# A six-layer cross network on one core: five named buffers, output in halves, first weights ahead of stores, and VectorE's sums interleaved

## The chip, the cores and the metric

One Trainium2 chip, one core. The metric is the device time of the program in microseconds, lower is better. The kernel before took 2305.39 us (median of three runs, 2305.22 to 2308.65).

## The reference, cut to what matters

```python
# x0: 16384 x 1024, ws: 6 x 1024 x 1024, bs: 6 x 1024, all bf16
x = x0
for l in range(6):
    proj = jnp.einsum('bd,de->be', x, ws[l]) + bs[l]
    x = x0 * proj + x
return x
```

Each row of x goes through the six layers by itself, so rows can be taken in any grouping; within a group the layers follow one another.

## The kernel before, in words

**Tiles.** The state is kept transposed in SBUF, features on partitions. A *pair* is 1024 rows, as two blocks n = 0, 1 of 512 rows, and the 1024 features are two halves of 512 (index `dh` of the input, `eh` of the output). A pair's x0 is a tile `x0T` (128 x 2 x 8 x 512), its running state a tile `xst` of the same size (2 MB each). There are 16 pairs.

**The product.** For one pair and one layer, the 2 x 2 blocks of rows and features are multiplied in Strassen's and Winograd's way: seven half-size products in place of eight. They are numbered 1 to 7, and so are their weight tiles (512 KB each): 1, 2 and 4 are blocks of the layer's matrix as it is, 5, 6, 3 and 7 are sums and differences of blocks. On the other side stand differences of state blocks: `T13` (one instruction that makes T[5] and T[7]), `T2` = T[6], `T4` = T[4]. From round 1 on, products 2 and 4 are split once more in the same way (`inner`, with the transformed weights 8 and 9, and with `ti2` and `ti4` on the side of the state).

**Loops.** Rounds s = 0 to 7 take two pairs each, sides A and B. Within a round, layers l = 0 to 5, and within a layer a *step* for A, then a step for B. PE's order in a step of rounds 1 to 7 is: product 1 (16 matmuls of 512 columns; after the first four the few matmuls that the previous step left over, `defer`), the inner products of 2 mixed in, product 5, product 3, product 6 with the inner products of 4, product 7. A step of round 0 has no inner products.

**VectorE.** It makes T13, T2, T4, ti2 and ti4, the sums of products that are C1 (output half 0) and C2 (output half 1), and then multiplies by x0 (`MULT`) and adds the old state (`ADD`) into `xst`. The sums for output half 1 of a step come in the next step, in `trail`: they are the *trail* of pair Y while PE works on pair X. Before, the sums of output half 0 are ended within the step itself (`fin`, called at the step's end for n = 1). ScalarE only empties PSUM.

**Weights.** In round 0, raw blocks come from HBM (`load_raw`), VectorE makes the combinations (`combo`, lines 117 to 130), and each is also stored to a buffer `Lc` in HBM. Later rounds load all nine tiles of a layer, in the order 1, 2, 8, 5, 3, 6, 4, 9, 7, from the input (1, 2, 4) or from Lc. They lie in a ring of 11 tiles, `wring`. The steps of side B ask for the loads (`weights`, which calls `prefetch_upto`, lines 92 to 97): when B uses the weight at place i, the one at place i + 10 is issued, and it waits until PE has ended with the tile that it replaces. Steps of side A issue none.

**The queue.** But for four weight loads at the start, which ScalarE issues, all DMAs are issued by SP, in one order: weights, x0 of new pairs (`load_x0`, a transposing DMA, line 198), and output. At the end of a pair `store_out` (line 248) transposes the 2 MB of state by one DMA back into the pair's own `x0T` tile (line 250), and then two DMAs of 1 MB write it to HBM in pieces of 256 bytes (line 254). `pin` keeps an instruction in the order in which the code gives it; what isn't pinned (before: weight loads, x0 loads, output and the stores to Lc) is placed by the scheduler. x0 tiles come from a pool of three, `xst` tiles from a pool of two. x0 of a new A pair is asked for at layer 2 of the round before, that of a new B pair in the step of A at layer 0 of its own round.

**The end.** The last pair isn't stored by DMA transposes: PE transposes its tiles, ScalarE and VectorE empty PSUM, and eight DMAs of 256 KB leave (`rows_out`, line 523).

Of the kernel before, what the change touches and what calls it, by code (L numbers as in the profile page):

```python
# [8 lines left out]
ADD = mybir.AluOpType.add  # L9
# [8 lines left out]
def kernel(  # L18
# [14 lines left out]
    NB = 512  # L33
# [28 lines left out]
    x0t_pool, xst_pool = pool("x0t", 3), pool("xst", 2)  # L62
# [4 lines left out]
    def wtile():  # L67
        return wring.tile([P, KH, H], BF16, name="wp")

# [20 lines left out]
    state = {"next": 0, "last_dma": None}  # L90

    def prefetch_upto(n):
        while state["next"] < min(n, len(keys)):
            k = keys[state["next"]]
            W[k] = wtile()
            state["last_dma"] = nc.sync.dma_start(W[k][:], raw_src(k[1], k[2]) if k[2] in RAW else lc(k[1], k[2]))
            state["next"] += 1

    def nosync(ins, before, reason):
        tc.add_manual_dep(ins.ins, before.ins.name,  # L100
                          mybir.DependencyInfo(mybir.DependencyClass.NoSync, mybir.DependencyReason.DATA),
                          reason=reason)

    raw12 = {}

    def load_raw(l, eng, pids):
        for pid in pids:
            if pid == 12:
                t = raw12[l] = ei_pool.tile([P, KH, H], BF16, name="ea")
            else:  # L110
                t = W[0, l, pid] = wtile()
            pin(eng.dma_start(t[:], raw_src(l, pid)))

    def combo(l, pid):
        if pid <= 7:
            a, op, b = {5: (lambda: raw12[l], ADD, lambda: W[0, l, 4]), 6: (lambda: W[0, l, 5], SUB, lambda: W[0, l, 1]),
                        3: (lambda: W[0, l, 2], SUB, lambda: W[0, l, 6]), 7: (lambda: W[0, l, 1], SUB, lambda: raw12[l])}[pid]
            t = ei_pool.tile([P, KH, H], BF16, name=("eb", "e4")[l % 2]) if pid == 5 else wtile()
            vtt(t[:], a()[:], b()[:], op)
            W[0, l, pid] = t  # L120
# [9 lines left out]
        nc.sync.dma_start(lc(l, pid), t[:])  # L130
# [4 lines left out]
    def inner_t(src, name):  # L135
        ti = ti_pool.tile([P, 4, 2, NQ], BF16, name=name)
        b = sub4(src)
        vtt(ti[:, 0], b[0, 1], b[0, 0], SUB)
        vtt(ti[:, 2], b[1, 1], b[0, 1], SUB)
        vtt(ti[:, 1], b[1, 1], ti[:, 0], SUB)  # L140
        vtt(ti[:, 3], b[1, 0], ti[:, 1], SUB)
        return ti
# [42 lines left out]
    x0T_A = x0t_pool.tile([P, 2, KD, NB], BF16, name="x0T")  # L185
    x0T_B = x0t_pool.tile([P, 2, KD, NB], BF16, name="x0T")
    xrows = [evt(), evt()] + [t_pool.tile([P, KH, NB], BF16, name=i) for i in ("T2", "T4")]
    for q in range(4):
        n, h = q // 2, q % 2
        pin(nc.sync.dma_start(xrows[q][:], x0[n * NB:(n + 1) * NB, h * H:(h + 1) * H].rearrange("(r p) d -> p r d", p=P)))  # L190
        if q == 0:
            pin(nc.sync.dma_start(b_rows[:], bs.rearrange("l (m p) -> (l m) p", p=P)))
    load_raw(0, nc.scalar, (1, 2, 12, 4))

    def load_x0(pr, x0T):
        for n in range(2):
            r0 = pr * PR + n * NB
            ti_ = nc.sync.dma_start_transpose(out=x0T[:, n], in_=x0[r0:r0 + NB, :])  # L198
            if state["last_dma"] is not None:
                nosync(ti_, state["last_dma"], "behind the weight loads already issued")  # L200

    load_x0(1, x0T_B)
    warm_in = const.tile([P, 1], BF16, name="warm_in")
# [25 lines left out]
    def trail(Y, prompt):  # L229

        if Y is None:
            return []
        C2 = Y.C2
        x0T, dst, src = Y.x0T, Y.xst, Y.src_in
        eh1 = lambda t: t[:, :, KH:KD, :]
        out = [lambda: vtt(C2[:, 1], Y.U3s[:], Y.P5s[:], ADD)]
        if Y.E4 is not None:
            def s4():
                e = Y.E4
                for i in range(2):  # L240
                    vtt(e[:, 2 * i:2 * i + 2, NQ:NB], e[:, 2 * i:2 * i + 2, (1 - i) * NQ:(2 - i) * NQ], Y.e5[:], ADD)
            out.append(s4)
            out.append(lambda: vtt(C2[:, 0], C2[:, 0], Y.E4[:], ADD))
        out.append(lambda: vtt(C2[:], C2[:], eh1(x0T), MULT))
        out.append(lambda: vtt(eh1(dst), C2[:], eh1(src), ADD))
        return out

    def store_out(Y):
        xo = Y.x0T[:].rearrange("p n k (j r) -> p (n k j) r", r=P)
        nc.sync.dma_start_transpose(out=xo, in_=Y.xst[:].rearrange("r n k b -> r (n k b)"))  # L250
        with nc.allow_non_contiguous_dma(reason="256B runs"):
            for n in range(2):
                r0 = Y.pr * PR + n * NB
                nc.sync.dma_start(out[r0:r0 + NB, :].rearrange("(j p) (k r) -> p k j r", p=P, r=P),  # L254
                                  Y.x0T[:, n].rearrange("p k (j r) -> p k j r", r=P))

    for s in range(NPAIR // 2):
        for l in range(L):
            for side in ("A", "B"):
# [6 lines left out]
                if l == 0:  # L266
                    X.xst = xst_pool.tile([P, 2, KD, NB], BF16, name="xst")
                if side == "A" and l == 0 and s > 0:
                    t = x0t_pool.tile([P, 2, KD, NB], BF16, name="x0T")
                    load_x0(X.pr + 1, t)  # L270
                    new["B"] = Pair(X.pr + 1, t)
                if side == "A" and l == 2 and s + 1 < NPAIR // 2:
                    t = x0t_pool.tile([P, 2, KD, NB], BF16, name="x0T")
                    load_x0(X.pr + 2, t)
                    new["A"] = Pair(X.pr + 2, t)

# [27 lines left out]
                half = lambda pt: (lambda m: pt[:, m * NQ:(m + 1) * NQ])  # L304
# [10 lines left out]
                todo = trail(Y, False)  # L315
# [10 lines left out]
                prompt = Y is not None and Y.l == L - 1  # L326
                own = []
                if not first:
                    own = [X.T2, X.T4]
                    if in4:  # L330
                        own.append(lambda: setattr(X, "ti4", inner_t(X.T[4], "ti4")))
                seq = todo + own if prompt else [f for pair in zip(todo + [None] * 9, own + [None] * 9) for f in pair if f is not None]
                for f in seq:
                    f()
                if prompt:
                    store_out(Y)
                if in2:
# [11 lines left out]
                    inner(half(q1), wr[0, 0], b[0, 0], True)  # L349
                    evi(ea[0, 0], q1)  # L350
                    inner(half(q5), wi[:, 0], ti[:, 0], True)
# [3 lines left out]
                    inner(half(q2), wr[1, 0], b[1, 0], True)  # L355
# [4 lines left out]
                    inner(half(q1), wi[:, 1], ti[:, 1], False)  # L360
                    evi(ea[0, 1], q1)
                    inner(half(q5), wi[:, 2], b[1, 1], False)
# [3 lines left out]
                    inner(half(q1), wi[:, 3], ti[:, 2], False)  # L366
                    evi(ea[1, 1], q1)
                    mm(5, w5, pX, 2, True)
                    inner(half(q1), wr[1, 1], ti[:, 3], False)
                    evi(ea[1, 0], q1)  # L370
                    ev(P5s, pX, 1)
                    ev(P5s, pX, 2)
                    w3 = weights(3)
# [11 lines left out]
                else:  # L385
# [24 lines left out]
                    for m in range(KH):  # L410
                        mm(5, w5, pX, m, True)
                        ev(P5s, pX, m)
                    w3 = weights(3)
# [17 lines left out]
                if need2 and not late:  # L431
                    N.ti2 = inner_t(N.rhs(2), "ti2")
                x0T, dst, src = X.x0T, X.xst, X.src

                def fin(Cb, eh, n):
                    xs = slice(eh * KH, (eh + 1) * KH)
                    vtt(Cb[:, n], Cb[:, n], x0T[:, n, xs, :], MULT)
                    return lambda: vtt(dst[:, n, xs, :], Cb[:, n], src[:, n, xs, :], ADD)

                fin(C1, 0, 0)()  # L440
                if s == 0:
                    if side == "A":
                        if l + 1 < L:
                            load_raw(l + 1, nc.sync, (12, 4, 1, 2))
# [10 lines left out]
                X.E4 = X.defer = None  # L455
                C2 = cb_pool.tile([P, 2, KH, NB], BF16, name="cb")
                X.C2, X.U3s, X.P5s, X.l, X.src_in = C2, U3s, P5s, l, src
                if in4:
# [9 lines left out]
                    inner(half(z1), wr4[0, 0], b4[0, 0], True)  # L468
# [3 lines left out]
                    inner(half(z5), wj[:, 0], t4[:, 0], True)  # L472
# [3 lines left out]
                    inner(half(z1), wj[:, 1], t4[:, 1], False)  # L476
# [5 lines left out]
                    inner(half(z1), wj[:, 3], t4[:, 2], False)  # L482
# [32 lines left out]
                fin(C1, 0, 1)()  # L515
                if need2 and late:
                    N.ti2 = inner_t(N.rhs(2), "ti2")
                if last:
                    final_tail = (X, C1, C2, U3s, P5s, psA, psX)
# [3 lines left out]
    X, C1, C2, U3s, P5s, psA, psX = final_tail  # L523
    def rows_out(pts, srcs, start, yo, n, eh, eng):
        for j in range(KH):
# [6 lines left out]
            if j % 2 == 1:  # L532
                r0 = X.pr * PR + n * NB + (j - 1) * P
                nc.sync.dma_start(out[r0:r0 + 2 * P, eh * H:(eh + 1) * H].rearrange("(j p) d -> p j d", p=P), yo[:, j - 1:j + 1, :])

    of_x = lambda n, eh: (lambda m, j: X.xst[:, n, eh * KH + m, j * P:(j + 1) * P])
    for h in range(2):
        hs = slice(2 * h, 2 * h + 2)
        vtt(C2[:, 1, hs, :], U3s[:, hs, :], P5s[:, hs, :], ADD)
# [5 lines left out]
    rows_out([bank(psX) for _ in range(KH)], of_x(0, 0), True, evt(), 0, 0, (1, 1, 1, 1))  # L545
    pT = [bank(psA) for _ in range(KH)]
    rows_out([bank(psX) for _ in range(KH)], of_x(1, 0), True, evt(), 1, 0, (1, 1, 1, 1))
# [33 lines left out]
```

## Time and profile before

| what | value |
|---|---|
| median of three runs | 2305.39 us |
| the profiled execution | 2303.93 us, its span 2302.1 us, mean granted clock 0.997 |
| PE, VectorE (DVE), ScalarE (ACT) busy | 98%, 95%, 83% of the span |
| matmuls of product 1 to 7 (L295), of inner products (L301) | 7829 of 512 columns, 4676 of 256 columns recorded |
| evictions of PSUM by ACT, 128 x 512 | 694 ns with bias, about 590 ns without |
| VectorE sums, 128 x 2048 and 128 x 4096 | 1.22 us, 2.29 us |
| DMA on SP's queue | 326.16 MB, 50.4% of 16 engines' span |
| weight load from Lc, from the input: issue to landing, median | 4.0 us, 5.3 us |
| output, 1 MB: issue to landing, median | 9.6 us |
| transposing DMA: x0 (1 MB), state (2 MB): issue to landing, median | 7.9 us, 11.7 us |

How to read it: busy shares are means over the whole span. Lines such as L46 or L295 are lines of helpers through which all sums or all matmuls go, so a group is known by its tiles: `T<-xst` is a difference of state blocks, `cb` a sum (C1 or C2), `wp` a weight, `px` PSUM. "SPq" is SP's sequencer, which issues DMAs. Some matmul records are missing, and a matmul's row lasts longer (379 ns) than the distance to the next one's start (216 ns).

### The profile page before, as it was taken

Reading aid. Unit: us, or ns where it says so; the run is one execution under the profiler, and the core shown is the slowest. Engines: PE = TensorE matmul, PEld = TensorE weight load, DVE = VectorE, ACT = ScalarE, POOL = GpSimd, SP = SyncE. Lnnn points to the kernel's source line nnn. Section 1 sums busy time; section 2 is a strip of 40 time slices with the busy share of each in tenths; the row PEclk is TensorE's granted clock in tenths of the full one; section 3 lists DMA queues with packets and bytes.
Section 4 is the critical chain, followed back from the end, with each engine's and each line's share of the span. In section 5 each row is a group of like instructions: output and inputs, shape, how many; then the busy total and the mean of one; then the engine's idle time right before and its main releaser. Section 6 shows DMA issues by size and latency. Waiting matters only on the chain.

```text
span 2302.1 us, 33220 instructions
## 1 busy us (share of the span) xinstructions
PE 2259.3 (98%) x12658; PEld 1258.0 (55%) x12909; DVE 2186.7 (95%) x2328; ACT 1912.4 (83%) x3294; POOL 0.7 (0%) x6
## 2 busy tenths in 40 slices
PE   8999999999999999999999999999999999999997
PEld 3444455555555555555555555555555555555554
DVE  5988889999999999999999999999999999999997
ACT  5777778888888888888888888888888888888886
POOL 0000000000000000000000000000000000000000
PEclk9999999999999999999999999999999999999999
DMA  8332295522954239532495234942349433582324
GB/s 247 133 115 100 111 210 163 149 83 86 243 175 128 83 105 245 177 106 92 115 264 161 83 111 121 268 132 92 120 125 260 119 117 112 138 229 94 121 98 110
DMA packets 495743, 330.38 MB, mean 144 GB/s; under 512 B 377824, under 2 KB 458720, under 8 KB 495584
## 3 DMA queue, kind: packets, MB, share of 16 engines
q1 hardware_dynamic: 493472, 326.16, 50.4%
q8 instruction: 101, 1.65, 0.3%
q10 hardware_dynamic: 2112, 2.10, 0.3%
q14 instruction: 58, 0.48, 0.1%
HBM read 212.87 MB, written 52.43 MB: 115 GB/s over the span
## 4 chain that ended last, share of the span: by engine, by line
PE 81%; DVE 7%; DMA 7%; SPq 2%; issue 1%; ACT 0%; DVEq 0%
PE px L295 63%; PE px L301 18%; DMA x0T<-xst 3%; DVE cb L46 3%; DMA out_dram<-x0T 3%; SPq L198 2%; DVE T L46 2%; DMA x0T<-in_x_dram 2%; DVE xst L46 1%; DVE ti L46 1%; DMA wp<-in_ws_dram 0%; DVE ea L46 0%; PE px L527 0%; SPq L254 0%; DVE e L46 0%
## 5 line engine op out<-in xcount | busy, mean ns | idle before, releaser
L295 PEld LDWEIGHTS <-wp 128*128 128x128 bf16 x7888 | 771.2, 98 | 742.1 <-DVE T L46 6.5
L295 PE MATMUL px<-T,wp 128*128 128x512 bf16 x4499 | 1111.6, 379 | 11.4 <-DVE T L46 4.8
L55 ACT ACTIVATE ev<-px,b_all 128x512 bf16<-128x512 f32 x1152 | 747.6, 694 | 93.7 <-PE px L295 85.8
L295 PE MATMUL px<-xst,wp 128*128 128x512 bf16 x2625 | 635.4, 379 | 4.9
L301 PEld LDWEIGHTS <-wp 128*128 128x128 bf16 x4676 | 457.2, 98 | 250.2 <-DMA wp<-in_ws_dram 1.6
L52 ACT CAST ev<-px 128x512 bf16<-128x512 f32 x828 | 477.6, 591 | 119.9 <-PE px L295 119.8
L46 DVE TENSOR_TENSOR cb<-cb,x0T 128x2048 bf16<-128x2048 bf16 (+2 forms) x291 | 454.4, 1562 | 4.6
L301 PE MATMUL px<-ti,wp 128*128 128x256 bf16 x2672 | 400.9, 273 | 0.0
L46 DVE TENSOR_TENSOR xst<-cb,xst 128x2048 bf16<-128x2048 bf16 (+1 forms) x240 | 378.2, 1576 | 9.2 <-PE px L527 0.5
L52 ACT CAST ea<-px 128x512 bf16<-128x512 f32 x336 | 196.6, 585 | 141.3 <-PE px L301 141.3
L46 DVE TENSOR_TENSOR cb<-ev 128x2048 bf16<-128x2048 bf16 (+1 forms) x205 | 248.8, 1214 | 30.5 <-ACT ev L52 30.1
L55 ACT ACTIVATE cb<-px,b_all 128x512 bf16<-128x512 f32 x384 | 244.4, 684 | 11.4 <-PE px L295 5.2
L52 ACT CAST e<-px 128x512 bf16<-128x512 f32 x332 | 195.3, 588 | 0.7 <-PE px L301 0.7
L46 DVE TENSOR_TENSOR T<-xst,T 128x2048 bf16<-128x2048 bf16 x160 | 195.0, 1219 | 0.8
L46 DVE TENSOR_TENSOR T<-xst 128x4096 bf16<-128x4096 bf16 x80 | 182.7, 2284 | 0.0
L52 ACT CAST eb<-px 128x512 bf16<-128x512 f32 x252 | 148.7, 590 | 6.3
L301 PE MATMUL px<-T,wp 128*128 128x256 bf16 x996 | 135.9, 273 | 0.7 <-DMA wp<-in_ws_dram 0.7
L295 PE MATMUL px<-x0T,wp 128*128 128x512 bf16 x516 | 126.0, 379 | 2.2 <-DMA x0T<-in_x_dram 0.4
L301 PE MATMUL px<-xst,wp 128*128 128x256 bf16 x840 | 126.0, 273 | 0.0
L46 DVE TENSOR_TENSOR cb<-ev,ea 128x2048 bf16<-128x2048 bf16 x84 | 102.9, 1225 | 11.1 <-ACT ev L55 2.6
L46 DVE TENSOR_TENSOR cb<-cb,e 128x2048 bf16<-128x2048 bf16 x83 | 101.2, 1220 | 1.3
L46 DVE TENSOR_TENSOR ea<-ea,eb 128x1024 bf16<-128x1024 bf16 (+1 forms) x168 | 85.7, 551 | 0.0
(49 smaller groups left out, 660.5 us busy)
## 6 DMA issues: line engine op xcount, KB each, us to landing
wp<-Lc SPq DMA_DIRECT2D x252, 512.0 KB, 4.0
wp<-in_ws_dram SPq DMA_DIRECT2D x141, 512.0 KB, 5.3
out_dram<-x0T SPq DMA_DIRECT2D x30, 1024.0 KB, 9.6
Lc<-wp SPq DMA_DIRECT2D x18, 512.0 KB, 2.7
Lc<-ti SPq DMA_DIRECT2D x12, 512.0 KB, 2.8
ea<-in_ws_dram SPq DMA_DIRECT2D x5, 512.0 KB, 4.5
out_dram<-ev SPq DMA_DIRECT2D x8, 256.0 KB, 3.2
wp<-in_ws_dram ACTq DMA_DIRECT2D x3, 512.0 KB, 7.2
```

The lines of the kernel that those rows point to most:

```text
L46: return pin(nc.vector.tensor_tensor(out=out, in0=in0, in1=in1, op=op))
L52: return pin(nc.scalar.copy(out=out, in_=in_))
L55: return pin(nc.scalar.activation(out=out, in_=in_, func=IDENT, bias=bias, scale=1.0))
L198: ti_ = nc.sync.dma_start_transpose(out=x0T[:, n], in_=x0[r0:r0 + NB, :])
L295: nc.tensor.matmul(pts[m][:], lhsT=wt[:, k, m * P:(m + 1) * P], rhs=rhs[:, k, :], start=(start and k == 0), stop=(k == KH - 1), **kw)
L301: nc.tensor.matmul(dst(m), lhsT=w[:, k, m * P:(m + 1) * P], rhs=rhs[:, k, :], start=(start and m == 0 and k == 0), stop=(k == 1), skip_gro ...
```

## The change

1. **Five buffers by name.** The pools of x0 and state tiles become five tiles `big0` to `big4`. A table `home` says which of them holds A's x0, B's x0, A's state, B's state and the next A's x0, and it turns from round to round: the next B's x0 takes A's old state tile, the next A's state takes A's old x0 tile.
2. **Earlier x0 of B.** It is loaded in the step of B at layer 5 of the round before.
3. **Output in two halves.** `store_half` takes output half 0 or 1: two transposing DMAs of 512 KB and eight stores of 128 KB. Half 0 is issued in the next step as soon as its last sum is made, half 1 (`end_of`) after product 5 of that step. The last pair's first quarter (n = 0, half 0) leaves in this way too.
4. **Pinned.** Weight loads, stores to Lc, x0 loads and output all keep the order of the code; the hint that put x0 loads behind weight loads (`nosync`) is gone.
5. **First weights ahead of stores.** Tiles of layers 0 and 1 are given out at the start (`alloc`), and weights 4, 1 and 2 of layer 1 are loaded right after x0 of pair 1. Weight 12 of layer 1 (single buffered) keeps its place.
6. **VectorE's order.** The sums of output half 0, n = 1 move from the step's end into the next step's trail, behind T13, and the trail alternates with T2, T4 and the four parts of `ti4`; `ti2` alternates with the first sums. At the last pair, C2's sum is made in one instruction in place of two.

```diff
-    x0t_pool, xst_pool = pool("x0t", 3), pool("xst", 2)
+    big = pool("big", 1)
+    def bigt(i):
+        return big.tile([P, 2, KD, NB], BF16, name=f"big{i}")
...
-            state["last_dma"] = nc.sync.dma_start(W[k][:], raw_src(k[1], k[2]) if k[2] in RAW else lc(k[1], k[2]))
+            pin(nc.sync.dma_start(W[k][:], raw_src(k[1], k[2]) if k[2] in RAW else lc(k[1], k[2])))
...
+    def alloc(l):
+        for pid in (1, 2, 4, 6, 3, 7):
+            W[0, l, pid] = wtile()
...
-        nc.sync.dma_start(lc(l, pid), t[:])
+        pin(nc.sync.dma_start(lc(l, pid), t[:]))
...
+    home = dict(xA=0, xB=1, sA=2, sB=3, nA=4)
+    x0T_A, x0T_B = bigt(0), bigt(1)
...
+    alloc(0)
+    alloc(1)
     load_raw(0, nc.scalar, (1, 2, 12, 4))
...
-            ti_ = nc.sync.dma_start_transpose(out=x0T[:, n], in_=x0[r0:r0 + NB, :])
+            pin(nc.sync.dma_start_transpose(out=x0T[:, n], in_=x0[r0:r0 + NB, :]))
     load_x0(1, x0T_B)
+    load_raw(1, nc.sync, (4, 1, 2))
...
+    def trail(Y, store):
+        m1, a1 = fin_of(Y, C1, 0, 1)
+        def a1s():
+            a1()
+            if store:
+                store_half(Y, 0)
+        return [m1, lambda: vtt(C2[:, 1], Y.U3s[:], Y.P5s[:], ADD), a1s,
+                s4 if E4 is not None else None,
+                (lambda: vtt(C2[:, 0], C2[:, 0], E4[:], ADD)) if E4 is not None else None,
+                lambda: vtt(C2[:], C2[:], eh1(Y.x0T), MULT),
+                lambda: vtt(eh1(Y.xst), C2[:], eh1(Y.src_in), ADD)]
...
-        nc.sync.dma_start_transpose(out=xo, in_=Y.xst[:].rearrange("r n k b -> r (n k b)"))
+    def store_half(Y, eh, ns=(0, 1)):
+        ks = half(eh)
+        for n in ns:
+            pin(nc.sync.dma_start_transpose(out=Y.x0T[:, n, ks, :].rearrange("p k (j r) -> p (k j) r", r=P),
+                                            in_=Y.xst[:, n, ks, :].rearrange("r k b -> r (k b)")))
+            for n in ns:
+                r0 = Y.pr * PR + n * NB
+                for j in range(KH):
+                    pin(nc.sync.dma_start(
+                        out[r0 + j * P:r0 + (j + 1) * P, eh * H:(eh + 1) * H].rearrange("p (k r) -> p k r", r=P),
+                        Y.x0T[:, n, ks, j * P:(j + 1) * P]))
...
+                    if side == "A" and s > 0:
+                        home = dict(xA=home["nA"], xB=home["sA"], sA=home["xA"], sB=home["sB"], nA=home["xB"])
+                    X.xst = bigt(home["s" + side])
-                if side == "A" and l == 0 and s > 0:
-                    load_x0(X.pr + 1, t)
+                def end_of(Y, ended):
+                    if ended:
+                        store_half(Y, 1)
+                        if side == "B" and s + 1 < NPAIR // 2:
+                            t = bigt(home["sA"])
+                            load_x0(Y.pr + 3, t)
+                            new["B"] = Pair(Y.pr + 3, t)
...
-                seq = todo + own if prompt else [f for pair in zip(todo + [None] * 9, own + [None] * 9) for f in pair if f is not None]
-                if prompt:
-                    store_out(Y)
+                for f in (m1, s11, a1, t2, s4, t4, e4, i02, mC2, i1, aC2, i3):
+                    if f is not None:
+                        f()
...
                     ev(P5s, pX, 2)
+                    end_of(Y, ended)
                     w3 = weights(3)
...
-                fin(C1, 0, 0)()
+                for f in (m0, a0) if late else (j02, m0, j1, a0, j3):
+                    if f is not None:
+                        f()
+                if last:
+                    store_half(X, 0, (0,))
-                            load_raw(l + 1, nc.sync, (12, 4, 1, 2))
+                            load_raw(l + 1, nc.sync, (12, 4, 1, 2) if l > 0 else (12,))
...
                 vtt(C1[:, 1], U2s[:], S53[:], ADD)
-                fin(C1, 0, 1)()
...
-    rows_out([bank(psX) for _ in range(KH)], of_x(0, 0), True, evt(), 0, 0, (1, 1, 1, 1))
```

## The prediction, made before the changed kernel had run

> **What bounds the kernel now.** I read the page's busy shares first, then PE's waits, then the stretches in which PE waited.
>
> ```profile
> PE 2259.3 (98%) x12658; PEld 1258.0 (55%) x12909; DVE 2186.7 (95%) x2328; ACT 1912.4 (83%) x3294; POOL 0.7 (0%) x6
> ```
>
> PE is the bound; its 512-column matmuls follow each other every 0.216 us (starts in the timeline), so a step is 112 x 0.216 = 24.2 us in round 0 and 108 x 0.216 = 23.4 us later. The diff leaves PE's stream as it is, but for 16 transposes at the end. So the change can act only through PE's waits:
>
> ```profile
> PE px L295 <- DVE T L46: 13.4, 8, 7.6
> ...
> PE px L301 <- DMA wp<-in_ws_dram: 0.7, 1, 0.7
> ...
> PE px L295 <- DMA x0T<-in_x_dram: 0.4, 1, 0.4
> ```
>
> (Who waited for whom: total us, times, longest.) One wait of 7.6 us is half of the T waits; the remaining T waits (0.95 in the first step, 4.8 in six later rounds) are short. The long one, first as VectorE and then as PE show it:
>
> ```profile
> 41.58 1.23 DVE L46 TENSOR_TENSOR e<-ea,wp 128x2048 bf16<-128x2048 bf16 x1 [11.43 <-DMA wp<-in_ws_dram]
> ...
> 49.31 2.28 DVE L46 TENSOR_TENSOR T<-x0T 128x4096 bf16<-128x4096 bf16 x1
> ```
> ```profile
> 51.65 4.54 PE L295 MATMUL px<-T,eb 128*128 128x512 bf16 x13 [7.63 <-DVE T L46]
> ```
>
> VectorE stood 11.4 us before a weight of layer 1, T13 of the second pair stood behind it, and PE behind T13.
>
> The other place is the change of pairs, where SP's one queue carries output, input and weights. SP's timeline at the change from round 2 to round 3 (start, length of the issue):
>
> ```profile
> 854.94 3.81 SPq L96 DMA_DIRECT2D wp<-Lc  x2
> 861.05 10.06 SPq L250 DMA_TRANSPOSE x0T<-xst  x1
> 871.21 0.99 SPq L96 DMA_DIRECT2D wp<-Lc  x2
> 874.24 4.95 SPq L254 DMA_DIRECT2D out_dram<-x0T  x2
> 879.28 4.70 SPq L96 DMA_DIRECT2D wp<-in_ws_dram  x1
> 884.07 1.35 SPq L96 DMA_DIRECT2D wp<-Lc  x2
> ...
> 886.05 13.58 SPq L198 DMA_TRANSPOSE x0T<-in_x_dram  x2
> ```
>
> Read by product number, step B of layer 5 (PE starts it at 849.98) queues: 8, 5, transpose T (2 MB), 3, 6, stores S (2 MB), 4, 9, 7, 1, input X (2 MB). Issues last as long as the data ahead of them: the queue is full and runs in order. How fast it drains, from the windows view (last two columns: DMA share, GB/s):
>
> ```profile
> 863.00:869.00 6.00, 5.95 (x34) 3.30 (x34) 5.72 (x13) 5.32 (x11) 0.00 (x0) 1.00 1.16 219
> 877.00:883.00 6.00, 6.00 (x40) 3.86 (x40) 5.83 (x7) 4.42 (x9) 0.00 (x0) 1.00 0.90 218
> 893.00:896.00 3.00, 2.95 (x16) 1.57 (x16) 2.96 (x3) 2.37 (x4) 0.00 (x0) 1.00 1.28 290
> 924.00:928.00 4.00, 4.00 (x26) 2.35 (x25) 4.00 (x3) 3.92 (x8) 0.00 (x0) 1.00 0.97 343
> ...
> 48.00:52.00 4.00, 0.35 (x1) 0.13 (x2) 3.96 (x4) 0.00 (x0) 0.00 (x0) 0.50 0.02 6
> ```
>
> The first four are T, S, X and weights: 1.05 MB of T or S takes 4.8 us, 2.1 MB of X 7.2, one weight (0.52 MB) 1.5. The fifth is the granted clock (1.00 above, 0.50 here) in the long wait.
>
> Step A of layer 0 then shows when its weights are due:
>
> ```profile
> 887.22 1.03 PE L295 MATMUL px<-T,wp 128*128 128x512 bf16 x4
> 888.97 0.61 PE L301 MATMUL px<-T,wp 128*128 128x256 bf16 x4 [0.72 <-DMA wp<-in_ws_dram]
> ```
>
> Weight 6 is due at 887.22 (13.9 us after the step's start at 873.36), 4 0.9 us later, 9 2.2, 7 some 4.8 us later. Weight 4, behind S, is already 0.9 us late. There is no slack here.
>
> **Part by part, against the profiled execution (2303.93 us; span 2302.1).**
>
> *Weights of layer 1 first.* In the built program SP now issues x0 of pair 1 and then weights 4, 1, 2 of layer 1, and the early load of pair 2 (two transposes, 4.3 and 5.7 us of SP) moves to layer 2. SP is through with pair 1 at 21.5; three weights, four stores of combinations and weight 12 are then 8 x 1.5 = 12 us behind the input that ends at about 23.5, so 12 lands near 36 instead of 41.5. Three combinations, C1's sum and T13 (4 x 1.2 + 2.3 = 7.1) end at 43.1, ahead of PE's 44.0. Two sums that stood ahead of T13 come after it. The wait goes: 7.6 + 0.16 (a matmul's row lasts 0.379, its successor starts after 0.216). The half clock cost 8 matmuls x 0.21 = 1.7 more. I take -9.2; if weight 12 lands at 39, T13 ends at 46.1 and 2.1 of the wait stay: -7.
>
> *Earlier input.* The B pair's X moves one step ahead, from behind S of A, into the old state buffer. The short waits of the six later rounds go: 4.8 + 0.7 + 0.4, and 0.16 for each of eight, together -7.3.
>
> *Output in halves, all pinned.* In the built program step B of layer 5 queues: 8, T half, 8 stores, 5, 3, T half, 8 stores, **X, and only then 6, 4, 9, 7, 1**. So four weights that stood at least partly ahead are now behind all of T, S and X. With the rates above, at the same change of pairs:
> - Weight 8 is issued at 854.94 when its slot is free, as before, and has arrived by about 857.6. VectorE has the first half's sums by about 854.4 (T13 starts 2.4 us earlier, then three sums), so T's start isn't set by them.
> - T half 4.8 + 0.5 between its two parts: 862.9. Stores: 0.5 until the first, then 4.8 by the rate or 8 x 0.77 = 6.2 by the pitch of the kernel's last eight stores; I take 5.5, as both rows are near: 868.9. Weights 5 and 3: 871.9. (VectorE has the second half ready at about 865.)
> - T half 5.3, stores 6.0: 883.2. X 7.2 + 0.5: 890.9. Weight 6: 1.5, and 0.8 to its signal: 893.2. Due at 887.22: **6.0 us late**. Weight 4 0.6 later still, 9 0.2; 7 is in time. So 6.8 us for each of the six changes after rounds 1 to 6: **+41**. With the stores at the rate and no pauses it is 2.9 (17 in all), with the pitch and 1 us more per transpose 10 (61).
>
> *The clock.* A 2.3 us wait at 1466 left the clock at 1.00; the 7.6 us wait brought 0.50 from 48.0 to 54.8 and cost 1.7. Six microseconds lies nearer to the second: 1.2 each, **+7** (0 to 15). The Trainium skill, "TensorE: Matmul & The Clock Gate", What's actually happening, says that the clock falls to half after one idle window of about 3.4 us, that windows run free of the program, and that a busy window must pass before it rises. The trace agrees so far: 6.8 us at 0.50 are two such windows. By that rule an estimate is a drop in three of four waits of 6 us, 3.4 to 6.8 us at half speed after each, so 1.9 us a wait, +12 in place of +7 and a sum 5 us higher.
>
> *First change of pairs* (round 0, step 24.2 us, one weight fewer behind X): T's first half starts near 289, and the same sum puts weight 4 within 1 us of its due time: +0.5 (0 to 3).
>
> *VectorE's interleaving.* T13 to T13 is 23.19 us, below PE's 23.38; dependent neighbours start 1.25 us apart (847.30, 848.55), independent ones 1.14. Interleaving shortens a chain that PE already hides: 0 (-1 to +1). What it moves back (state sums behind T13) is due only in the pair's next step. The cover is 0.19 us a step; VectorE 0.3 us slower than now would cost 84 x 0.1.
>
> *The end.* One quarter of the last pair leaves by transpose, so 16 PE transposes, four evictions and two stores go. But SP, not PE, ends the kernel (last eight stores 2288.4 to 2298.4, end 2302.1). From 2264, T, S, T, S, a quarter and six stores by the same rates end at 2300 to 2301: 0 (-2 to +2).
>
> *Five named buffers* add no instruction, but a wait: the new A pair's first state sum writes where A's stores read. They have left by about 884; the sum is due on VectorE near 893 (846.2 in a step that PE starts at 826.6, so 19.5 after 873.4). Behind it stand C1's second sum and the next T13, with 5 us to spare: 0.
>
> Sum: -9.2 - 7.3 + 41 + 7 + 0.5 = **+32**, that is 2336 us beside 2303.93. The median of the runs shown is 1.5 above the profiled execution: **2337**.
>
> **Rivals.**
> - *The queue drains faster than I add it up* (no pauses, stores overlap T): 1 to 4 us late and no clock loss, 17 in all: 2303.9 - 16 + 17 + 1.5 = 2306. For it: S's share is only 0.90. Against: T and X run with a share above 1, and 0.9 us late is where the kernel stands already.
> - *Weights in time, faster:* only the removed waits count: 2305.4 - 16.5 = 2289. The mechanism is the early start of T (855.3 instead of 861.05), which gives the queue 5.8 us; it decides if T, S, X and two weights take under 27.3 us from 857.6 (887.2 less 2.3 for weight 6). By the rates alone they take 4 x 4.8 + 7.2 + 3 = 29.4.
> - *The lateness spreads:* the B pair's T and S follow the late weights, and weights 2 and 8 of layer 1 come behind those, near 924 and 925 by the same sum. They are due near 930 (step A of layer 1 starts at 927); with 6 us more on the queue they add a wait of their own to each change: 2370 or more. That is my sum at its upper ends.
> - *The first wait stays* because weight 12 still comes after the stores: 9 us more than the forecast, in its range.
>
> **Chances.** Forecast 0.68 (own range 2314 to 2365), faster queue 0.15, in time 0.12, spreading 0.05. The range 2300 to 2365 leaves out the last two. About 0.2% (4.6 us) is what a measurement of this kernel can tell from no change: below 2300.8 I put 0.14 (in time, and a little of the faster queue), within 0.09, above 0.77.
>
> **What would show it.** PE's waits list weights from Lc or ws, near 6 us, six times, in step A of layer 0 at the first matmul with weight 6; SP's timeline has X directly ahead of these loads; PEclk falls below 1.00 there. The wait of 7.6 at 51.65 is gone. I am wrong if PE waits under 2 us at the changes of pairs, if weight 12 of layer 1 lands after 39, or if SP's issues of the small stores or half transposes take other times than those used.

## The result, and the profile after

| | before | after |
|---|---|---|
| median, same chip | 2306.68 us (4 runs) | 2333.3 us (4 runs, 2330.51 to 2333.93) |
| the profiled execution | 2303.93, span 2302.1 | 2330.51, span 2328.7 |
| mean granted clock | 0.997 | 0.991 |

The changed kernel takes 1.0113 times as long (95% interval 1.0095 to 1.013). The profiled executions differ by 26.6 us; the prediction's sum was +32 and its time 2337.

Busy time of each engine, from the page of the kernel after:

```profile
PE 2265.7 (97%) x12642; PEld 1259.0 (54%) x12893; DVE 2144.3 (92%) x2327; ACT 1909.6 (82%) x3290; POOL 0.7 (0%) x6
```

VectorE fell from 95% to 92%, and PE, which bounds the kernel, from 98% to 97%: an engine was relieved that was not the bound, and the bound now stands idle longer. For what, the waits of PE say (who waited for whom: total us, times, longest):

```profile
PE px L331 <- DMA wp<-Lc: 35.9, 6, 7.9
...
PE px L331 <- DVE T L46: 1.0, 1, 1.0
```

The 13.4 us of waits for T are 1.0 now, and six waits for weights from Lc have come, one at each change of pairs after rounds 1 to 6.

**A change of pairs.** SP's timeline of the kernel after, step B of layer 5 in round 2 (PE starts it at 845.96; start, length of the issue):

```profile
851.35 6.70 SPq L277 DMA_TRANSPOSE big<-big  x2
858.14 4.53 SPq L283 DMA_DIRECT2D out_dram<-big  x8
...
864.02 8.12 SPq L277 DMA_TRANSPOSE big<-big  x2
872.34 4.46 SPq L283 DMA_DIRECT2D out_dram<-big  x8
876.84 8.97 SPq L213 DMA_TRANSPOSE big<-in_x_dram  x2
885.91 0.53 SPq L99 DMA_DIRECT2D wp<-Lc  x1
886.54 0.38 SPq L99 DMA_DIRECT2D wp<-in_ws_dram  x1
```

The last two lines are weights 6 and 4. SP reaches them only when it is through with all of X, at 885.91. PE's timeline of the same kernel there (the wait and what ended it in brackets):

```profile
889.53 3.29 PE L331 MATMUL px<-T,wp 128*128 128x512 bf16 x8 [6.18 <-DMA wp<-Lc]
892.66 0.60 PE L337 MATMUL px<-T,wp 128*128 128x256 bf16 x4
```

The first line is the first matmul with weight 6, the second the first with weight 4. Eight matmuls of 512 columns took 3.29 us; at the distance of 0.216 us, with the longer last row, it would be 1.9. The windows view says why (the third and second numbers from the end are clock and DMA share):

```profile
886.00:892.00 6.00, 2.47 (x6) 0.89 (x7) 2.90 (x3) 0.55 (x1) 0.00 (x0) 0.50 1.01 304
```

Around the end of the wait the clock is 0.50. A DMA share at 1 says that the queue wasn't idle: it carried what stood ahead. Between the first use of weight 6 and that of weight 4 lie eight matmuls here and four in the kernel before (887.22 in the prediction): at the six late changes the changed kernel runs another order on PE.

**The start.** VectorE's timeline of the kernel after, then PE's:

```profile
35.94 1.23 DVE L46 TENSOR_TENSOR e<-ea,wp 128x2048 bf16<-128x2048 bf16 x1 [5.78 <-DMA ea<-in_ws_dram]
...
40.74 2.28 DVE L46 TENSOR_TENSOR T<-big 128x4096 bf16<-128x4096 bf16 x1
```

```profile
43.88 3.62 PE L331 MATMUL px<-T,eb 128*128 128x512 bf16 x16
```

T13 of the second pair ends at 43.0 (before: 51.6), and PE starts on it at 43.88 without a wait.

**Where the time went.** A wait is taken as the distance of two matmul starts less 0.216; clock losses are half of the time at 0.50 that fell behind each wait.

| term | forecast, us | measured, us |
|---|---|---|
| wait and half clock at the start | -9.2 | -9.4 |
| short waits at the earlier changes of rounds | -7.3 | -7.4 |
| weights late, six changes | +41 | +36.9 (4.1, 6.3, 5.9, 5.9, 8.1, 6.6) |
| half clock behind them | +7 | +10.9 (six of six) |
| first change of pairs | +0.5 | 0 |
| the end, last 512-column matmul to the last DMA | 0 | -3.9 (18.1 to 14.2) |
| sum, with some -0.5 not placed | +32 | +26.6 |

### The profile page after: what moved, and what is told of

It reads as the page before. It is cut to its first block, busy times and chain, and to the rows that moved or that the text cites. A ratio compares the mean times of both kernels' runs of the same rounds, so it can differ in the third digit from the quotient of the medians.

```text
span 2328.7 us, 33550 instructions
## 1 busy us (share of the span) xinstructions
PE 2265.7 (97%) x12642; PEld 1259.0 (54%) x12893; DVE 2144.3 (92%) x2327; ACT 1909.6 (82%) x3290; POOL 0.7 (0%) x6
## 4 chain that ended last, share of the span: by engine, by line
PE 86%; DVE 5%; SPq 4%; DMA 3%; issue 2%; ACTq 0%; DVEq 0%
PE px L331 67%; PE px L337 19%; SPq L213 2%; DVE cb L46 2%; SPq L283 1%; DMA wp<-Lc 1%; DVE big L46 1%; DVE T L46 1%; DMA big<-big 1%; DVE ti L46 1%; DMA wp<-in_ws_dram 1%; SPq L277 0%; DVE ea L46 0%; DVE e L46 0%; DVE ev L49 0%
## 5 line engine op out<-in xcount | busy, mean ns | idle before, releaser
L331 PE MATMUL px<-T,wp 128*128 128x512 bf16 x4499 | 1120.1, 382 | 42.4 <-DMA wp<-Lc 35.9
L331 PE MATMUL px<-big,wp 128*128 128x512 bf16 x3141 | 761.5, 379 | 6.6 <-ACT big L52 0.2
L46 DVE TENSOR_TENSOR cb<-cb,big 128x2048 bf16<-128x2048 bf16 (+2 forms) x291 | 454.2, 1561 | 0.8
L46 DVE TENSOR_TENSOR big<-cb,big 128x2048 bf16<-128x2048 bf16 (+1 forms) x288 | 453.1, 1573 | 1.9
L46 DVE TENSOR_TENSOR cb<-ev 128x2048 bf16<-128x2048 bf16 x204 | 248.9, 1220 | 62.0 <-ACT ev L52 62.0
L46 DVE TENSOR_TENSOR T<-big 128x4096 bf16<-128x4096 bf16 (+1 forms) x97 | 220.2, 2270 | 81.7 <-PE px L331 80.6
L55 ACT ACTIVATE cb<-px,b_all 128x512 bf16<-128x512 f32 x384 | 244.4, 684 | 10.9 <-PE px L331 7.6
L46 DVE TENSOR_TENSOR T<-big,T 128x2048 bf16<-128x2048 bf16 x192 | 234.3, 1221 | 1.3
L337 PE MATMUL px<-big,wp 128*128 128x256 bf16 x1008 | 151.2, 273 | 0.0
L46 DVE TENSOR_TENSOR ti<-big,ti 128x512 bf16<-128x512 bf16 x168 | 70.6, 420 | 0.2
```

The costliest lines, as they stand in the source:

```text
L46: return pin(nc.vector.tensor_tensor(out=out, in0=in0, in1=in1, op=op))
L55: return pin(nc.scalar.activation(out=out, in_=in_, func=IDENT, bias=bias, scale=1.0))
L331: nc.tensor.matmul(pts[m][:], lhsT=wt[:, k, m * P:(m + 1) * P], rhs=rhs[:, k, :], start=(start and k == 0), stop=(k == KH - 1), **kw)
L337: nc.tensor.matmul(dst(m), lhsT=w[:, k, m * P:(m + 1) * P], rhs=rhs[:, k, :], start=(start and m == 0 and k == 0), stop=(k == 1), skip_gro ...
```

## The experiments

The theory: X stands ahead of weights that are due sooner, and that alone makes the kernel slower; the other parts gain. The rivals: the total number of bytes is too much in any order; the clock is only a mark and costs nothing of its own; halves or the interleaving matter more.

### X behind the weights

In `end_of`, X of the next B pair is no longer loaded; it is loaded at the end of the same step, behind weights 6, 4, 9, 7 and 1.

```diff
                         store_half(Y, 1)
-                        if side == "B" and s + 1 < NPAIR // 2:
-                            t = bigt(home["sA"])
-                            load_x0(Y.pr + 3, t)
-                            new["B"] = Pair(Y.pr + 3, t)
...
+                if ended and side == "B" and s + 1 < NPAIR // 2:
+                    t = bigt(home["sA"])
+                    load_x0(Y.pr + 3, t)
+                    new["B"] = Pair(Y.pr + 3, t)
                 X.src = X.xst
```

> The changed kernel, with one thing moved: the x0 load of the next B pair (X) is issued behind the weight loads 6, 4, 9, 7, 1 of the same step, not ahead of them. Theory (the order on SP's queue): the six waits for weight 6 (36.9 us by the distances of matmul starts) and the half clock behind them (about 11 us) go, 2333.3 - 36.9 - 10.9 = 2285.5; X now lands about 8 us later, just in time for T13 of B, up to 1 us late each time: 2285 to 2292. Rival (the output in many small DMAs, or its place in the queue, makes the weights late whatever X does): most of the waits stay, over 2315.

Measured: 2285.14 us beside 2303.06 of the kernel before, ratio 0.992 (0.9905 to 0.9934). SP's timeline and PE's waits of this kernel:

```profile
867.59 4.67 SPq L283 DMA_DIRECT2D out_dram<-big  x8
872.36 0.47 SPq L99 DMA_DIRECT2D wp<-Lc  x1
872.92 0.39 SPq L99 DMA_DIRECT2D wp<-in_ws_dram  x1
...
874.95 13.57 SPq L213 DMA_TRANSPOSE big<-in_x_dram  x2
```

```profile
PE px L327 <- DVE T L46: 1.4, 2, 1.0
...
PE px L327 <- DMA big<-in_x_dram: 0.3, 1, 0.3
```

Weight 6 is issued at 872.36 in place of 885.91, no wait for a weight is left and the mean clock is 0.999. X itself is late at one change: PE waits 0.3 us for it and then 0.4 for the T13 that had waited for it. The same bytes in another order are 1.9% of the time: the theory holds, and the bytes as such are not the limit.

### Half of X behind them

Only the second of X's two transposing DMAs goes behind the weights.

```diff
-                            load_x0(Y.pr + 3, t)
+                            load_x0(Y.pr + 3, t, (0,))
...
+                if ended and side == "B" and s + 1 < NPAIR // 2:
+                    load_x0(Y.pr + 3, new["B"].x0T, (1,))
```

> The changed kernel with only the second half of X (n = 1, 1 MB) moved behind the weight loads; the first half stays ahead. Theory: lateness follows the bytes ahead of weight 6, so the mean wait of 6.1 us falls by the 3.6 to 4.1 us of 1 MB to 2.0 to 2.5, six times 12 to 15 us, and as a 2.3 us wait left the clock whole before, no half clock: 2285.5 + 14 = 2299, between 2296 and 2306. Rival (any transposing input between output and weights costs its start, not its bytes): the waits stay near 6 us, over 2322.

Measured: 2301.45 us beside 2303.06, ratio 0.9989 (0.998 to 0.9999). PE's waits:

```profile
PE px L331 <- DMA wp<-Lc: 9.1, 5, 4.3
PE px L337 <- DMA wp<-in_ws_dram: 2.9, 5, 1.0
```

Half of X is 3.6 us by the rate in the prediction, and 4.5 by SP's issue of X in the kernel after (8.97 for both halves). By PE's starts the waits at weight 6 are 11.0 us, 1.8 a change in place of 6.1: 4.3 less. So the lateness follows the bytes ahead. The second line is new, and makes 14.7 in all with the first: weight 4 is late at five of the six changes. This kernel has four matmuls between the two weights again. Only one change, that with a wait of 4.5 us, has a clock of 0.50; it is the one at which weight 4 isn't late.

### The wait filled with matmuls

PE gets 18 matmuls of zeros (18 x 0.216 = 3.9 us) ahead of product 6 in step A of layer 0, from round 2 on. They go into the bank `z5`, which an inner product of weight 9 overwrites later.

```diff
+                    if side == "A" and l == 0 and s > 1:
+                        for _ in range(18):
+                            nc.tensor.matmul(z5[:], lhsT=zero[:, 0:P], rhs=zero[:], start=True, stop=True)
                     mm(6, w6, pA, 0, False)
```

> The changed kernel with 18 matmuls of zeros (18 x 0.216 = 3.9 us) into a free PSUM bank ahead of product 6, in step A of layer 0 of rounds 2 to 7, where PE waits 4.1 to 8.1 us for weight 6. They do no part of the result. Theory (the waits cost twice: their own length, and half clock after them): the weights come no later, the idle stretches fall to 0.2 to 4.2 us, the clock stays at 1.00 in most of them, 2333.3 - 11 = 2322, 2320 to 2326. Rival (the half clock in the record costs nothing, or comes from elsewhere): 2333, 2331 to 2336.

Measured: 2325.99 us, ratio 1.01 (1.0083 to 1.0117). Work was added and the time didn't grow (2333.3 for the kernel after): the zeros lie in the wait, of which PE's waits show what is left:

```profile
PE px L331 <- DMA wp<-Lc: 9.4, 6, 2.5
```

Spells at 0.50 are three of 3.4 us, where the kernel after has six, four of them 6.8 us long. The span is 2322.9 us in place of 2328.7, the sign and size that a clock with a price of its own should give; by the medians the two intervals overlap, so the stronger evidence for the price is the row above, eight matmuls in 3.29 us. The drops weren't done away with: three came at idle times of 2.0 to 2.7 us. The other three changes kept a clock of 1.00, though weight 6 came 4.7 to 5.1 us after the last matmul ahead of the zeros; in the kernel after, every wait of 4.1 us or more dropped it. So the zeros counted as work for the clock.

### Layer 1's first weights back behind the stores

Weights 4, 1 and 2 of layer 1 go back to their old place. Pair 2's input stays in layer 2, and all is pinned.

```diff
-    load_raw(1, nc.sync, (4, 1, 2))
...
-                            load_raw(l + 1, nc.sync, (12, 4, 1, 2) if l > 0 else (12,))
+                            load_raw(l + 1, nc.sync, (12, 4, 1, 2))
```

> The changed kernel with weights 4, 1 and 2 of layer 1 loaded where the kernel before loaded them, behind the four stores of combinations and behind weight 12; all stays pinned, so the load of pair 2 remains at layer 2. Theory of the prediction (the early place of these loads ends the first wait of 7.6 us and its half clock): the wait comes back, 2333.3 + 9.4 = 2343, 2339 to 2344. Rival (what ended the wait is that pair 2's two input DMAs, 2 MB or 7 to 8 us of the queue, no longer stand ahead): weight 12 then lands near 32 and 2 near 37, the combinations end near 39 as now, 2333, 2331 to 2336.

Measured: 2331.41 us, ratio 1.012 (1.0105 to 1.0136), against 1.0113 with the weights early. VectorE's timeline:

```profile
33.00 1.23 DVE L46 TENSOR_TENSOR e<-ea,wp 128x2048 bf16<-128x2048 bf16 x1 [2.60 <-DMA wp<-in_ws_dram]
...
38.27 2.29 DVE L46 TENSOR_TENSOR T<-big 128x4096 bf16<-128x4096 bf16 x1
```

The wait at the start doesn't come back; T13 even starts 2.5 us sooner. So the early weights didn't end it. This part of the theory fell.

### Pair 2's input at the start again

On top of "X behind": pair 2's two input DMAs go back to the start, and layer 1's weights are in their old place.

```diff
-    load_raw(1, nc.sync, (4, 1, 2))
+    x0T_2 = bigt(home["nA"])
+    load_x0(2, x0T_2)
```

> The version with X behind the weights (2285.1), with pair 2's two input DMAs at the start again, ahead of the stores and of layer 1's weights, and these weights in their old place: the queue of the kernel before at the start, but VectorE's new order. Theory (these 2 MB ahead made the first wait): weight 12 and 4 land near 41.5, T13 stands 2.4 us earlier than before, so a wait of 5 us and about 1.5 for the half clock: 2291, 2289 to 2293. Rival (the wait went because T13 no longer stands behind the two sums): 2285 to 2287.

Measured: 2293.59 us, ratio 0.9941 (0.9927 to 0.9955), against 0.992 without. VectorE's timeline, then PE's:

```profile
42.62 1.23 DVE L46 TENSOR_TENSOR e<-ea,wp 128x2048 bf16<-128x2048 bf16 x1 [12.55 <-DMA wp<-in_ws_dram]
```

```profile
50.40 5.92 PE L329 MATMUL px<-T,eb 128*128 128x512 bf16 x16 [6.46 <-DVE T L46]
```

The wait is back, 6.5 us long, with a spell of 6.8 us at half clock, of which 4.7 fall behind it. With the run before, which took away the weights alone and kept the gain, this names the cause: 2 MB of input that nobody needs until round 1, ahead of weight 12. Whether early weights would help with pair 2's input at the start wasn't tried.

### Whole output in place of halves

On top of "X behind": one transposing DMA of 2 MB and two stores of 1 MB, at the place of `store_half(Y, 1)`; the earlier output of half 0 is left out.

```diff
-                        store_half(Y, 1)
...
+                        store_out(Y)
```

> The version with X behind the weights (2285.1), with the output of a pair in one transposing DMA of 2 MB and two stores of 1 MB again, issued where half 1 is issued now. Theory (one queue drained at the rates of the windows): T can start only when the last sum is made, about 15 us into the step, so weight 6 comes about 1.7 us late and X about 1.3 us late for T13, 3 to 4 us for each of six changes: 2300 to 2310. Rival (the halves bring nothing, only X's place matters): 2285, 2283 to 2288.

Measured: 2334.32 us, ratio 1.0123 (1.0109 to 1.0137): slower as expected, but by some 47 us (0.0203 of 2305), not by 15 to 25. SP's timeline and PE's waits:

```profile
860.80 9.67 SPq L287 DMA_TRANSPOSE big<-big  x1
873.26 4.89 SPq L291 DMA_DIRECT2D out_dram<-big  x2
878.25 4.75 SPq L99 DMA_DIRECT2D wp<-Lc  x1
```

```profile
PE px L334 <- DMA wp<-Lc: 12.0, 4, 3.6
PE px L334 <- DVE cb L46: 7.5, 2, 4.4
```

SP comes to weight 6 (third line) 32.7 us after the step's T13, as in "X behind" (32.9), but its issue lasts 4.75 us in place of 0.47: the 2 MB of stores, given out since 873.26, are still ahead of it. By PE's starts there are six waits at weight 6, of 2.8 to 4.6 us; the view puts two of them down to a sum (second line), at the same matmul, but there too weight 6 landed last (600.11 and 888.00, PE went on at 600.15 and 888.05). Of the 47 us, 37 are waits (28, of which 20 at weight 6 and the rest short ones elsewhere) and five half-clock spells (1.7 each) up to the last 512-column matmul, and 11 are at the end, where the last pair's first quarter stands behind the whole store of pair 14 (25.5 us in place of 14.2). The step I had missed is the end. This is not the order of the kernel before, whose whole output started earlier in its step.

### VectorE's old order

On top of "X behind": sums of output half 0 are ended in their own step again, and T2, T4 and the parts of `ti2` and `ti4` stand as before. Half 0's output is then issued as the next step's sums begin.

```diff
-                for f in (m1, s11, a1, t2, s4, t4, e4, i02, mC2, i1, aC2, i3):
...
+                seq = todo + own if ended else [f for q in zip(todo, own + [None] * (5 - len(own))) for f in q]
+                for f in seq:
...
-                for f in (m0, a0) if late else (j02, m0, j1, a0, j3):
+                for f in (m0, a0) if late else (j02, j1, j3, m0, a0):
...
+                for f in fin_of(X, C1, 0, 1):
+                    f()
```

> The version with X behind the weights (2285.1), with VectorE's old order: the sums of output half 0, n = 1 at the step's end, ahead of T13, and no alternation beyond that of the kernel before. Theory (PE's 23.38 us a step hide VectorE, and T13 at the changes waits for X, not for sums): 2285, 2283 to 2288. Rival (VectorE's busy time fell from 2187 to 2144 us by the interleaving, and at 95% busy that is worth something): 2289 or more.

Measured: 2282.05 us, ratio 0.9895 (0.9881 to 0.9908). VectorE is busy 2187.3 us again (2142.7 with the new order), a wait of 1.7 us is back at the second pair's first T13, and the kernel isn't slower but tends to be faster. Neither side had that. SP's timeline shows the place; first the new order, then the old:

```profile
2257.77 5.77 SPq L277 DMA_TRANSPOSE big<-big  x2
```

```profile
2255.35 4.47 SPq L275 DMA_TRANSPOSE big<-big  x2
```

The interleaving makes the chains shorter for VectorE but puts T2 and T4 between the last sums of an ended pair. Pair 14's second half is issued 2.4 us later, though the last 512-column matmul starts 1.5 us sooner, and the end takes 14.2 us in place of 10.4.

### The last quarter by PE

On top of "X behind": the last pair's first quarter leaves by PE's transposes again.

```diff
-                if last:
-                    store_half(X, 0, (0,))
...
+    rows_out([bank(psX) for _ in range(KH)], of_x(0, 0), True, evt(), 0, 0, (1, 1, 1, 1))
```

> The version with X behind the weights (2285.1), with the last pair's first quarter transposed by PE again and stored by two DMAs of 256 KB, as in the kernel before. The stretch from the last 512-column matmul to the end was 18.1 us before and is 14.2 now. Theory (the gain is that pair 15's output finds the queue empty, as pair 14's went out in two halves; the quarter's transpose now waits until 2319 in the queue and holds four stores): without it the end comes 1 to 3 us earlier, 2282 to 2284. Rival (the gain is the quarter that leaves early): 3 to 4 us later, 2288 to 2289.

Measured: 2281.51 us, ratio 0.9893 (0.9879 to 0.9906); the end takes 11.3 us. Sending the quarter by DMA is no gain in this kernel: the end is 14.2 us with it and 11.3 without. The 3.9 us that the kernel after saves at the end came from elsewhere, most likely from the queue being emptier when the last stores come, with pair 14 leaving in halves.

### Where the end's time lies

Two kernels, and beside them the changed kernel once more, unaltered. First, on top of "X behind", the sums of output half 0 are ended in their own step at layer 5 only:

```diff
+                if l == L - 1 and not last:
+                    for f in fin_of(X, C1, 0, 1):
+                        f()
```

> The version with X behind the weights (2285.1), and at layer 5 the sums of output half 0, n = 1 are ended in the step itself, as in the kernel before, so that the second transposing DMA of half 0 has its data when the first has gone; elsewhere the new order. Theory (in the version with the old order of sums, 2282.0, the gain was that SP no longer stood some 3 to 4 us at that DMA, in the last pair above all: 10.4 us from the last 512-column matmul to the end in place of 14.2, against 1.7 us lost at the first T13): both gains together, 2280 to 2282. Rival (the gain of the old order was a shorter sum chain in every step): 2285.

Measured: 2286.09 us, ratio 0.991 (0.9895 to 0.9925). The end takes 13.7 us: the theory fell. Half 0 was not what came late.

> The changed kernel once more, unaltered, on the same chip as the version beside it, so that the two are compared on one chip: 2333, 2330 to 2336; waits for weight 6 of 34 to 38 us in all.

Measured: 2336.6 us, ratio 1.0134 (1.0114 to 1.0153), 0.6 above the range, with six waits for weights of 37.0 us in all by PE's waits (35.9 in the first trace of this kernel).

The second goes on from the first: in the step behind a pair's last layer, all that is left of its sums comes ahead of T2 and T4.

```diff
-                for f in (m1, s11, a1, t2, s4, t4, e4, i02, mC2, i1, aC2, i3):
+                for f in (a1, s11, s4, e4, mC2, aC2, t2, t4, i02, i1, i3) if ended else (
+                        m1, s11, a1, t2, s4, t4, e4, i02, mC2, i1, aC2, i3):
```

> The version with X behind the weights and half 0 ended early (2286.1, 0.991 of the kernel before), and in the one step behind a pair's last layer all of that pair's remaining sums stand ahead of T2 and T4, as in the kernel before; elsewhere the new order. Theory (half 1's transposing DMA waits for the pair's last sum, which the new order makes some 4 us later: 10.9 us ahead of the last 512-column matmul against 14.1 with the old order): the stretch from that matmul to the end falls from 13.7 to about 10.4, 3 us less, with the first T13 still in time: ratio 0.988 to 0.990, 2278 to 2284. Rival (it was the old order in the other steps): ratio 0.991 or more.

Measured: 2280.57 us beside 2305.16, ratio 0.9895 (0.9879 to 0.9912); the end takes 11.0 us. SP's timeline:

```profile
2255.27 4.48 SPq L278 DMA_TRANSPOSE big<-big  x2
```

Half 1 now goes at 2255.27, 13.0 us ahead of the last 512-column matmul (2268.25); it was 10.2 in "X behind" and 10.9 in the first of the two. What set the end was the last sum of half 1. This kernel beats the kernel before by 1.05%. Those with VectorE's old order or with the last quarter by PE can't be told from it.

## Why the prediction came out right, point by point

- **Output in halves, all pinned (+41, measured +36.9).** Right in place, size and reason. Counted from PE's start of step B, weight 6 was forecast at 43.2 us and PE went on at 43.6; it was due at 37.2 in both. The waits at weight 6 are 6.1 us in the mean (6.0 forecast), and "X behind" takes them all away. The steps on the way erred both ways: T's first half was issued 5.4 us after PE's start of the step (7.6 forecast) and weights 5 and 3 were given out by 18.0 (21.9), but the second half with its stores took 12.8 us of SP (11.3 forecast), X 9.0 (7.7), and weight 6 went on to PE 3.6 us after its issue (2.3). That these errors, up to 3.9 us each, cancel to 0.4 is luck.
- **Weight 4 and weight 9 (0.8 a change).** This term didn't come, and the failed step is "the diff leaves PE's stream as it is". Weight 4 did land 1.4 to 2.3 us behind weight 6 (602.79 behind 600.89, 891.78 behind 889.48), and four matmuls of weight 6 take 0.9. But at the six late changes PE has eight of them ahead of weight 4's first, not four, and behind most waits PE ran at half clock besides: weight 4's first matmul starts 2.1 us after weight 6's at 600.94, nearly at full clock, and 3.1 at 889.53. With four between, as in "half of X behind", the lateness shows at the five changes at full clock. The weights' term was 4.1 too high and the clock's 3.9 too low; that their sum, 48, is so near to the 47.8 measured is luck.
- **The clock (+7, measured +10.9).** Mis-sized. I took 1.2 for each wait of 6 us; all six dropped the clock, at 1.4 to 2.6 each. The estimate from the Trainium skill, "TensorE: Matmul & The Clock Gate", What's actually happening, was +12, and the trace agrees with it better than with my value, though it gives a drop in three waits of four and all six came. That rule speaks of an idle window; in these traces a stretch with 2.1 us of idle time was enough (last section), and a wait of 6 us leaves more than that in one stretch wherever it falls.
- **The start (-9.2, measured -9.4).** The size was right and the reason wrong. The failed step is "weights of layer 1 first": the working named both that move and pair 2's input leaving the start, and gave the gain to the two together under that name. Two runs show that the second alone brings it: "layer 1's first weights back behind the stores" has no wait without the early weights, and "pair 2's input at the start again" has it back. The early weights put T13 2.5 us later, which VectorE's new order makes good: with the old one 1.7 us of the wait are back.
- **Earlier input (-7.3, measured -7.4).** Right in size: no wait for x0 or for T at the changes of rounds is left. That the earlier load alone brought it is argued, not shown; no run takes it away by itself.
- **The end (0, measured -3.9).** Mis-sized: 4 us off, outside its bounds of -2 to +2. I let the small stores run at a pitch of 0.77 us (0.57 measured) and found the queue fuller than it was; which of the two weighs more stays open. Of the parts, "the last quarter by PE" says that the quarter by DMA put 2.9 us on the end, so the rest of the change took some 6.8 off it.
- **VectorE's interleaving (0).** Right for the steps: 45 us less busy time (2142.7 beside 2187.3) moved nothing but the first T13. I had looked for its price only on PE; the sums that it pushes back are due to SP, and that costs 3 to 4 us at the end.
- **The rivals.** "Weights in time" gave 2289 for a kernel in which only the removed waits count. "X behind" is nearly that kernel: 17.9 us less than the kernel before beside it, where 16.5 was given. The profiled executions differ by 20.0, and the end's 3.9, which I had put at 0, is in that. "The lateness spreads" didn't happen: no wait at layer 1 in the list. "The first wait stays" didn't either: VectorE had weight 12 by 35.9.

## What to carry to other kernels

On a queue that runs in order, the place of a transfer is worth as much as its size: put what is due first ahead, and bulk that is due a step later behind it; here the same bytes were worth 1.9% of the time. Pinning an order takes away the scheduler's mixing, so write down each transfer's due time before pinning. Relieving an engine that was not the bound gained nothing here, and its new order may delay another consumer, which is seen only by asking who waits for each moved result.

## What the runs showed of the hardware

- The clock dropped behind a wait of only 4.1 us, and 1.3 us after that wait had ended: PE went on at 600.94 and the clock fell at 602.26, for 3.4 us. With filled waits it fell at idle times of 2.0, 2.4 and 2.7 us, while idle times of up to 1.8 us left it at 1.00 there and in "half of X behind", and one of 2.4 us in the kernel before did too. No fixed length of the wait decides it.
- What decides can be counted from these traces, though no run was made to test it. Within a trace the drops begin whole multiples of 3.4133 us apart: in the kernel after at 602.26, 885.56, 1175.69, 1465.83, 1752.55 and 2042.68, which are 83, 85, 85, 84 and 85 of them. Cut into such stretches, the traces show 29 drops from the second step to the last, each at the end of a stretch in which PE stood for 2.1 us or more (counted by the distances of matmul starts, less 0.216 or 0.109 for the matmul itself). Up to 1.99 us in a stretch brought none, and four stretches of 2.01 to 2.15 brought none either. The wait of 4.1 us that ended at 600.94 put 2.0 into one stretch and 2.1 into the next, at whose end the clock fell; the one of 2.4 us in the kernel before was cut into 1.6 and 0.9, and the clock stayed.
- In these traces an issue on SP lasts as long as the data ahead of it takes: weight 6 took SP 0.47 us behind stores of 128 KB given out over 4.67 us, and 4.75 us behind two of 1 MB given out over 4.89. At the 218 GB/s of the prediction's second window row, 1 MB takes 4.8 us and 2 MB 9.6.
